# A block-sparse attention feeding a squared-ReLU MLP: the second of four batches moved from masked dense scores to gathered blocks, with its transposes and the first batch's masks on TensorE

## The chip, the core and the metric

One core of a Trainium2 chip runs the whole program in one launch. The metric is the device time in microseconds; the kernel before was timed three times and its median is 258.22 us. TensorE (PE in the profile, PEld for its weight loads), VectorE (DVE), ScalarE (ACT), GpSimd (POOL) and SyncE (SP) each work through a queue of their own, in order.

## The reference

For each of 4 batches and 8 heads there are 768 queries and keys of 64 numbers, in 24 blocks of 32. A query block may look at its neighbours, at the first and the last block and at three blocks drawn at random; the first and the last query block look at everything. The result goes through a two-layer MLP (512 to 2048 to 512).

```
scores = scale * np.matmul(q, k.transpose(0, 1, 3, 2))
mask = np.abs(blk_i - blk_j) <= window
mask = mask | (blk_i == 0) | (blk_j == 0) | (blk_i == n_blocks - 1) | (blk_j == n_blocks - 1)
for qb in range(n_blocks):
    for kb in sampled_blocks[qb]:
        mask[qb * block:(qb + 1) * block, kb * block:(kb + 1) * block] = True
scores = np.where(mask, scores, -1000000000.0)
attn = np.exp(scores - max); attn = attn / sum          # by row
x = np.matmul(attn, v) as [B * S, H * D]
out = np.maximum(x @ w_in, 0.0) ** 2 @ w_out
```

All matrix products run in bf16; the inputs and the output are float32.

## The kernel before

The work is cut into tasks: small functions that issue a few instructions each. A string, `PROGRAM`, lists every task in the order in which it is issued, with its engine as a letter (P, V, A, G, S for PE, DVE, ACT, POOL, SP) and its number; `P283/1` is task 283 on TensorE with accumulator 1 of the four PSUM accumulators `X`. A planner outside the kernel wrote that string. Each engine runs its own tasks in the order of the string, so a task that waits holds up all that stands behind it on its engine. `T_` makes a task, with the tasks that it depends on (`deps`) and the buffers that it takes and gives back.

A *unit* `u` is two heads of one batch; units 0 to 3 are batch 0, 4 to 7 batch 1, and so on. `load` (SP queue) brings queries, keys and values of a unit, `cast_qk` and `cast_v` make bf16 of them. Queries and keys are needed with the 64 numbers of a head on the partitions: for batch 0 `transp` does this on TensorE (12 small transposes for a whole unit) and `evac` copies the result out of PSUM; for the later batches `transp_dma` does it with a DMA transpose from the SP queue (line 312).

Attention exists in two forms, chosen by `SB`, the number of dense batches (2 before).

*Dense* (`attend`, batches 0 and 1): a slot is one unit, 256 queries and 256 keys. `scores` issues 4 matmuls of 256 columns (line 203; `pair` issues two matmuls that use the upper and the lower 64 rows of the array at the same time), `exps` is one ACT instruction of 128x1024 (line 360), and `masks` multiplies by a 0/1 mask on DVE (line 367). For the first 256 queries of batch 0 the mask is instead added to the scores on TensorE (`add`: 4 more matmuls, with `oh` and `R2`), since the mask tiles are not there yet. `MASKED` lists the query ranges for which `mask_tile` (TensorE) and `mask_evac` build these mask tiles. Then `values` or `values_full` multiply by V, `normalize` divides by the row sum, and the result is transposed into `xT` for the MLP: on TensorE in batch 0 (`x_transp`, `x_evac`), by DMA in batch 1 (`x_transp_dma`, line 440).

*Gathered* (`visit`, batches 2 and 3): a visit handles two groups of 64 queries, for the four units of a batch, against only the keys that the groups may see, 384 for each group. `k_gather` copies the drawn key blocks together on DVE or POOL (lines 593 to 599; block numbers are read into registers by `load_blocks`), `v_store` writes V of the batch to DRAM, `v_window` (lines 552, 556) and `v_gather` (line 579 as an indirect DMA from POOL, line 582 from SP) bring the needed rows back. `s_scores`, `s_exps` (line 623), `s_masks` (line 630), `s_values` (line 653), `s_normalize` (lines 659, 662) follow, and `s_transp` (line 666) is a DMA transpose into `xT`. Which keys, and the small masks `MKS`, are worked out once by `table_slots`, `table_spread`, `table_rows` and `table_masks`; `table_slots` is one long DVE task and `table_rows` ends by loading the block numbers of all engines.

The MLP runs in 12 tiles of 256 tokens: `hidden` (8 matmuls of 256 columns), `relu` on ACT or DVE, `square` on ACT or POOL, `output` (8 matmuls, mostly of 512 columns), `out_copy`, `store`. These tasks are laid between the attention tasks to keep TensorE busy. The weights are brought by eight `w_load` tasks on the POOL queue (pieces 0 to 3 are `w_in`, 4 to 7 `w_out`); two `loads_gate` tasks on the SP queue hold back the loads of batch 1 until pieces 6 and 7 have landed.

Of the kernel before, what the change touches and what calls it, by code (L numbers as in the profile page):

```python
# [19 lines left out]
P = 128  # L20
# [5 lines left out]
def kernel(  # L26
# [34 lines left out]
    SB, VR, KG_BUFS, VG_BUFS = 2, D + 2, 2, 3  # L61
# [404 lines left out]

    def table_places(e):
        G.iota(before, pattern=[[1, SL - 4], [-1, SL]], base=4, channel_multiplier=0, **small)
        G.iota(ids[:, 0:4], pattern=[[1, 4]], base=0, channel_multiplier=2, **small)
        G.iota(bl, pattern=[[1, 2]], base=1, channel_multiplier=2, **small)  # L470
        G.memset(ids[:, 4:5], 0.0)
        G.memset(ids[:, 5:6], float(nb - 1))
        for i in range(P // block):
            G.iota(lane[i * block:(i + 1) * block], pattern=[[0, 1]], base=0, channel_multiplier=1, **small)

    def table_slots(e):
        tmp = RT[tb["tmp"][0].at]
        n = SL - 4
        tri, eq = (tmp[0:GR, i * n * SL:(i + 1) * n * SL].rearrange("g (s z) -> g s z", z=SL) for i in range(2))
        al, sm = (tmp[0:GR, 2 * n * SL + i * 2 * SL:2 * n * SL + (i + 1) * 2 * SL].rearrange("g (a s) -> g a s", a=2) for i in range(2))  # L480
        same = tmp[0:GR, 256:256 + 2 * SL * n_rand].rearrange("g (a s r) -> g a s r", a=2, r=n_rand)
        low[0] = RT[tb["tmp"][1].at][0:D].bitcast(BF)[:, 0:5 * P].rearrange("g (s c) -> g s c", c=P)
        V.tensor_copy(out=tab.rearrange("o (g s) -> o g s", s=TS)[:, :, 0:RS],
                      in_=sb_r[:, 2 * n_rand:2 * n_rand * (nb - 1)].rearrange("o (g s two) -> o g s two", g=GR, two=2)[:, :, :, 0])
        V.memset(low[0], 0.0)
        V.tensor_copy(out=ids[:, 6:SL], in_=sb_g.rearrange("g (s two) -> g s two", two=2)[:, :, 0])
        V.tensor_tensor(out=eq, in0=ids[:, 4:SL, None].broadcast_to([GR, n, SL]), in1=ids[:, None, :].broadcast_to([GR, n, SL]), op=AOP.is_equal)
        V.scalar_tensor_tensor(out=eq, in0=before, scalar=0.0, in1=eq, op0=AOP.is_gt, op1=AOP.mult)
        V.tensor_reduce(out=dup, in_=eq, axis=AX.X, op=AOP.max)
        V.tensor_tensor(out=al, in0=ids[:, None, :].broadcast_to([GR, 2, SL]), in1=bl[:, :, None].broadcast_to([GR, 2, SL]), op=AOP.subtract)  # L490
        V.tensor_scalar(out=sm, in0=al, scalar1=-1.0, scalar2=None, op0=AOP.is_ge)
        V.scalar_tensor_tensor(out=al, in0=al, scalar=1.0, in1=sm, op0=AOP.is_le, op1=AOP.mult)
        V.tensor_tensor(out=same, in0=ids[:, None, :, None].broadcast_to([GR, 2, SL, n_rand]),
# [5 lines left out]
        V.tensor_scalar(out=dup, in0=dup, scalar1=-1.0, scalar2=1.0, op0=AOP.mult, op1=AOP.add)  # L499
        V.tensor_tensor(out=al[:, :, 4:SL], in0=al[:, :, 4:SL], in1=dup[:, None, :].broadcast_to([GR, 2, n]), op=AOP.mult)  # L500
        def spread(j, of):
# [8 lines left out]
        V.tensor_scalar(out=half, in0=lane, scalar1=float(HB), scalar2=-float(HB), op0=AOP.is_ge, op1=AOP.mult)  # L510
        V.tensor_tensor(out=lane, in0=lane, in1=half, op=AOP.add)
# [11 lines left out]
    def table_rows(e):  # L523
        V.tensor_scalar(out=idx, in0=low[1][:, P:P + GR], scalar1=float(HB), scalar2=lane, op0=AOP.mult, op1=AOP.add)
        load_blocks("POOL")
        load_blocks("DVE")
        load_blocks("SP")

    def table_masks(g0, g1, e):
        n = g1 - g0  # L530
        for c in range(3):
            copy(e, MKS[:, g0:g1, c].rearrange("p g (e a i) -> p (g e) a i", e=2, a=2) if 0 else MKS[:, g0:g1, c].rearrange("p g (e a i) -> p g e a i", e=2, a=2),
# [36 lines left out]
    def load_blocks(e):  # L569
        for g in wanted[e]:  # L570
# [94 lines left out]
    def s_transp(b, v, e):  # L665
        sy.dma_start(out=x_tile(b, v // 2 * QW)[:, :, v % 2 * P:v % 2 * P + P], in_=xtile.pop(("s", b, v)).rearrange("p a h d -> p (a h d)"), transpose=True)
# [129 lines left out]
    def prepare(u):  # L796
# [4 lines left out]
        if u >= HP:  # L801
# [5 lines left out]
            for w in (1, 0):  # L807
# [4 lines left out]
                x = T_(transp_dma, u, w, deps=[c] + old_s, put=[qc])  # L812
# [74 lines left out]
    def visit(b, v, vw, acts):  # L887
# [4 lines left out]
        parts = [T_(v_gather, b, v, i, deps=[vw, cl, tb["rows"], tb["slots"]]) for i, g in enumerate(VISITS[v]) if g]  # L892
# [4 lines left out]
        for g in [g for g in VISITS[v] if g]:  # L897
            kc[g] = T_(k_gather, b, v, g, get=[] if kc else [kb], deps=[ev[u][1, 0] for u in us] + [tb["slots"]] + list(kc.values()))
# [17 lines left out]
        nm = T_(s_normalize, b, v, deps=[va], get=[xs], put=[yb, ot])  # L916
        mu["s", b, v] = T_(s_transp, b, v, deps=[nm] + x_get(b, v // 2 * QW), put=[xs])
# [26 lines left out]
    for us in [range(b * HP, (b + 1) * HP) for b in range(B)]:  # L944
        for u in us:
            prepare(u)
        mine = [a for a in order if a[0] in us]
# [14 lines left out]
        for a in mine:  # L962
            attend(a, us[0] < HP and a[1] == 0)

    sq_of, gbuf = {}, {}
    for T in TILES:
# [3 lines left out]
        for f in range(0, NF, n_u):  # L970
# [4 lines left out]
            for part in range(parts):  # L975
# [4 lines left out]
                             put=[xb[b, c0]] if f + n_u == NF and end else []))  # L980
# [21 lines left out]
        A29 G35 P4/3 V32 P30/0 P12/2 P14/3 P9/1 P5/1 V31 P33/1 V111 P36/3 P0/2 A37 V1 V34 P102/2 V209 V46 P47/0 P106/1 A103 V48 P104/3  # L1002
        V43 A107 P44/0 G57 P7/2 V45 A105 P58/1 V54 P113/0 V59 P55/2 A114 P117/3 G41 V56 P2/1 V67 A118 P115/2 V3 P108/0 A116 V64 P127/1
        V109 P10/3 P65/3 A128 P123/2 V66 A124 P68/1 P125/3 G75 V69 V63 P92/1 P110 A126 P133/2 G76 V112 A134 P137/3 G52 S28 S42 S18 S19
        V93 S20 P88/0 A138 G38 V155 V89 P84/1 P119/2 G74 V85 A60 P86/0 P39/3 P135/1 V120 G73 A87 V40 A136 P121 P61/0 G49 P129/3 V122
        V62 G77 V70 P176/2 P170/0 P139/1 A177 G81 V130 G80 A171 V140 P146/2 P131 V132 A147 P149/3 V172 P71/0 P141 V142 A150 V72 P50/2
        P173/1 V148 P781/0 A174 P782 V178 P189/3 P783 V51 A190 V175 P90/1 P15/2 P96/2 P784 V91 A97 P183/3 V151 A785 P94/2 P179/1 V95
        A184 G787 P143/0 P774/2 V180 P775 A144 V191 G78 P186/3 P181 P776 V182 A187 P777 V145 P157/0 V778 A786 P152/3 A158 P160/1 V188
        P788/2 A161 V153 P163/0 P789 V185 A164 P790 V162 P154 P217/1 P791 A156 V159 A218 P192/0 V165 P795/3 A792 V193 S82 P166/1 S83
        V296 V219 S53 S254 A779 G794 S253 P194 P100/2 A780 P796 V195 V167 A101 P214/0 P797 G793 A215 P168 P798 V169 P211/2 V799 P824/1  # L1010
        G79 A212 P825 P196/0 G256 V216 P826 A197 P199/3 P818/2 G801 S257 P827 A200 P819 V828 P202/0 A800 S261 P228/3 P820 G22 A203
        S262 P821 V213 P812/1 S269 A229 V822 P813 G258 P220/0 A829 P814 V201 P245/2 S259 P221 A246 V198 P815 P802/3 V222 A816 P231/2
        V266 P223 P803 A232 V204 S267 P239/1 V230 P804 A224 A240 V264 S270 P242/0 P205/2 V233 S265 A243 P225/1 P206 P805 V207 A226
        S277 V274 P288/0 S436 S255 P208 P806 V227 A289 S275 V247 P11/1 P291/1 A823 P234/0 V241 P807 A292 V210 V244 P98/2 P235 V272
        P808 A99 V236 A817 S273 P298/2 V290 P248/1 P237 A299 P809 V238 S278 V293 P285/0 S279 V300 P249 A810 P830/2 V250 P831 A286 V282
        P304/3 P251 P832 V260 A305 P301/0 V252 P833 S263 V287 P852/1 A302 S334 S283 V834 P853 P846/3 G280 P313/0 V303 P854 A314 P316/2
        S281 P855 P847 A317 V856 G284 P294/0 P848 A835 S271 P295 V306 P310/1 S21 P849 G268 V297 A311 P864/2 V318 P865 S440 A850 P307/0
        V315 P866 S438 A857 P308 G851 S446 P355/3 P867 V309 A356 P322/1 V868 P858/0 P859 A323 P349/3 V357 P325/2 P860 A350 V312 P861
        P836/1 V276 A326 V351 S456 P319/3 A862 P328/2 V327 S439 P320 S447 A329 V321 P352/0 P837 S811 V324 A353 S454 P339/2 V330 P838
        A340 V354 P331/3 P342/0 A869 S385 V341 P332 P358/2 V333 P839 A343 V23 S335 G441 P359 A863 P336/3 P361/0 G443 P840 A337 P841  # L1020
        G451 A362 S622 P364/3 G449 P842 A365 P373/0 G445 S450 P843 A374 G461 P870/3 A844 S444 P367/0 V338 P871 A368 V344 S463 P872
        V347 V360 S455 V366 S442 P376/0 P345/1 A377 V363 P379/2 P346 P873 S452 V348 A380 V369 P403/0 P874 A404 V375 S464 P370/2 V378
        P400/1 P393/0 V381 P371 A401 P875 V372 S471 S448 A394 V402 P382/1 P390/2 V405 P383 A391 P387/0 P876 V384 A388 V395 S386 P406/1
# [65 lines left out]
```

## Time and profile before

| | |
|---|---|
| median of 3 runs (range) | 258.22 us (257.47 to 258.88) |
| time of the profiled run, its span | 258.88 us, 257.1 us |
| TensorE busy | 243.1 us, 95% of the span, 5265 matmuls |
| ACT, DVE, POOL busy | 183.6 us, 171.3 us, 98.8 us |
| TensorE clock granted | full speed in every slice |
| dense part: 72 `exps`, 60 `masks` | 70.6 us of ACT, 40.9 us of DVE |
| gathered part: 56 `s_exps`, 48 `s_masks` | 41.6 us of ACT, 27.6 us of DVE |
| DMA | 47.08 MB, mean 183 GB/s |

"Busy" is the time in which at least one instruction of the engine is running by the records. Matmuls are pipelined: the record of one lasts 190 to 376 ns while the next starts much earlier. The pace of TensorE is therefore read from the starts of successive rows, not from the mean duration.

### The profile page before, as it was taken

What the parts mean: (1) busy time and instruction counts of PE and PEld (TensorE: products, weight loads), DVE (VectorE), ACT (ScalarE), POOL (GpSimd) and SP (SyncE); (2) the same over time, 40 slices, a digit from 0 to 9 for tenths busy, and PEclk for the clock granted to TensorE, in tenths of its full rate; (3) what the DMA queues carried; (4) which work ended last, traced back from release to release, by engine and by line L of the source; (5) the groups of instructions that cost most, each with busy time, mean ns of one, the idle gap of its engine ahead of it and who ended that gap; (6) DMA issues with size and microseconds to landing.
All of it is one profiled execution on the core that took longest, in us unless ns stands there. A gap on an engine that the chain in (4) does not pass through costs nothing.

```text
span 257.1 us, 12061 instructions
## 1 busy us (share of the span) xinstructions
PE 243.1 (95%) x5265; PEld 182.1 (71%) x5265; DVE 171.3 (67%) x408; ACT 183.6 (71%) x217; POOL 98.8 (38%) x178
## 2 busy tenths in 40 slices
PE   7888999999999997998998999999999999999993
PEld 4667879678874677975864867866875677767683
DVE  7778988899889995969916756657536725730301
ACT  3899999998999797846783975675965286623640
POOL 3183247003316026198556314264357620412100
PEclk9999999999999999999999999999999999999999
DMA  6999989999999996999699779998474923044022
GB/s 200 374 250 207 206 205 155 270 202 252 250 281 179 197 202 153 340 229 154 188 243 202 194 174 167 251 214 199 129 206 95 189 40 60 5 121 148 23 86 83
DMA packets 64692, 47.08 MB, mean 183 GB/s; under 512 B 31567, under 2 KB 60624, under 8 KB 64640
## 3 DMA queue, kind: packets, MB, share of 16 engines
q1 hardware_dynamic: 58512, 37.82, 64.7%
q0 software_dynamic: 5440, 8.05, 16.8%
q8 instruction: 41, 0.67, 1.1%
q10 hardware_dynamic: 688, 0.46, 0.6%
q14 instruction: 11, 0.09, 0.1%
HBM read 35.51 MB, written 7.91 MB: 169 GB/s over the span
## 4 chain that ended last, share of the span: by engine, by line
PE 53%; DVE 5%; DVEq 1%; issue 1%; ACT 1%; ACTq 0%
PE X L203 49%; PE X L653 4%; DVE VB L123 1%; ACT pT L623 1%; DVEq L561 1%; DVE MKS L123 1%; DVE pT L630 1%; DVE r L709 0%; DVE KG L599 0%; DVE qc L123 0%; DVE XS L413 0%; DVE KG L593 0%; DVE XS L662 0%; DVEq L599 0%; DVE rs L410 0%
## 5 line engine op out<-in xcount | busy, mean ns | idle before, releaser
L203 PE MATMUL X<-xT,w_in_sb 64*128 64x256 bf16 x1536 | 100.8, 269 | 2.8 <-issue 1.5
L203 PE MATMUL X<-w_out_sb,g 64*128 64x512 bf16 (+3 forms) x960 | 95.2, 334 | 0.1
L203 PEld LDWEIGHTS <-w_in_sb 64*128 64x128 bf16 x1536 | 74.6, 94 | 16.0 <-issue 5.4
L360 ACT ACTIVATE pT<-X 128x1024 bf16<-128x1024 f32 x72 | 70.6, 1030 | 7.6 <-PE X L203 6.8
L623 ACT ACTIVATE pT<-X 128x768 bf16<-128x768 f32 (+1 forms) x56 | 41.6, 766 | 26.5 <-PE X L203 23.9
L203 PEld LDWEIGHTS <-g 64*128 64x128 bf16 x960 | 40.3, 94 | 26.3 <-PE X L203 0.4
L720 POOL TENSOR_TENSOR g<-r 128x1024 bf16<-128x1024 f32 (+1 forms) x20 | 31.6, 1587 | 64.4 <-ACT r L707 47.2
L707 ACT ACTIVATE r<-X 128x1024 f32<-128x1024 f32 x28 | 29.8, 1068 | 20.6 <-PE X L203 20.5
L709 DVE TENSOR_SCALAR r<-X 128x1024 f32<-128x1024 f32 x20 | 24.5, 1224 | 26.7 <-PE X L203 13.7
L367 DVE TENSOR_TENSOR pT<-pT,VG 128x1024 bf16<-128x1024 bf16 x60 | 40.9, 715 | 0.2
L718 ACT ACTIVATE g<-r 128x1024 bf16<-128x1024 f32 (+1 forms) x40 | 35.2, 899 | 2.7 <-DVE r L709 2.5
L203 PE MATMUL X<-QKT 64*128 64x256 bf16 (+1 forms) x384 | 31.6, 250 | 3.3 <-DVE XS L413 1.3
L630 DVE TENSOR_TENSOR pT<-pT,MKS 128x768 bf16<-128x768 bf16 (+1 forms) x48 | 27.6, 607 | 10.7 <-ACT pT L623 10.5
L203 PEld LDWEIGHTS <-QKT 64*128 64x128 bf16 x384 | 16.7, 95 | 9.5 <-issue 4.1
L579 POOL DMA_INDIRECT VG<-rows,idx x19 | 20.2, 1061 | 4.4 <-issue 2.6
L203 PEld LDWEIGHTS <-pT 64*128 64x128 bf16 x768 | 16.0, 94 | 1.9
L203 PE MATMUL X<-VB,pT 64*128 64x65 bf16 x768 | 17.1, 190 | 0.0
L203 PEld LDWEIGHTS <-KG 64*128 64x128 bf16 x528 | 13.8, 95 | 4.5 <-issue 0.2
L659 DVE RECIPROCAL ss<-X 128x8 f32<-128x8 f32 x12 | 2.5, 206 | 19.5 <-PE X L653 17.3
L653 PEld LDWEIGHTS <-pT 128*64 128x64 bf16 x624 | 11.9, 111 | 4.9 <-issue 3.7
L203 PE MATMUL X<-QKT,KG 64*128 64x64 bf16 x528 | 15.3, 190 | 0.1
L123 POOL CAST VB<-vs 128x768 bf16<-128x768 f32 x9 | 7.8, 869 | 16.5 <-DMA vs<-in_v_dram 16.4
(107 smaller groups left out, 210.3 us busy)
## 6 DMA issues: line engine op xcount, KB each, us to landing
vs<-in_v_dram SPq DMA_DIRECT2D x14, 384.0 KB
ks<-in_k_dram SPq DMA_DIRECT2D x13, 384.0 KB
qs<-in_q_dram SPq DMA_DIRECT2D x12, 384.0 KB
out_dram<-ys SPq DMA_DIRECT2D x9, 512.0 KB
VG<-rows SPq DMA_DIRECT2D x20, 132.0 KB
w_in_sb<-in_moe_w_in_dram POOLq DMA_DIRECT2D x4, 512.0 KB, 8.6
w_out_sb<-in_moe_w_out_dram POOLq DMA_DIRECT2D x4, 512.0 KB, 9.9
rows<-VB SPq DMA_DIRECT2D x2, 792.0 KB
```

The costliest lines, as they stand in the source:

```text
L123: (V if e == "DVE" else G).tensor_copy(out=out, in_=in_)
L203: last = nc.tensor.matmul(out(r ^ crossed), lhsT(r ^ crossed, rows), rhs(r ^ crossed, rows), skip_group_check=True, **kw)
L360: A.activation(out=pT[:, :, 0:n], in_=stile.pop(a)[:, :, 0:n], func=AF.Exp, scale=scale)
L367: V.tensor_tensor(out=pT, in0=pT, in1=m[:, None].broadcast_to([P, 2, len(cs), w]), op=AOP.mult)
L579: G.indirect_dma_start(out=to[0:RS * HB], out_offset=None, in_=pairs, in_offset=bass.IndirectOffsetOnAxis(ap=idx[0:RS * HB, g - 1:g], axis=0))
L623: A.activation(out=pT[:, :, 0:n], in_=stile.pop((u, v, gs))[:, :, 0:n], func=AF.Exp, scale=scale)
L630: V.tensor_tensor(out=pT, in0=pT, in1=m[:, None].broadcast_to([P, 2, n]), op=AOP.mult)
L653: nc.tensor.matmul(po[i * D:(i + 1) * D, h, a * VW:(a + 1) * VW], pts[g][:, h, c * D:(c + 1) * D], val, start=a == 0 and c == 0, stop=c == ...
L707: A.activation(out=to, in_=src, func=AF.Relu)
L709: V.tensor_scalar(out=to, in0=src, scalar1=0.0, scalar2=None, op0=AOP.max)
L718: A.activation(out=g, in_=r, func=AF.Square)
L720: (G if e == "POOL" else V).tensor_mul(out=g, in0=r, in1=r)
```

## The change

- `SB` goes from 2 to 1: batch 1 runs in the gathered form, so 36 dense slots go (36 `scores` and `exps`, 36 `masks`, 24 `values` tasks, 12 `normalize`) and six visits come (28 `s_scores` and `s_exps`, 24 `s_masks`, 6 each of `s_values`, `s_normalize`, `s_transp`, 11 `k_gather`, 11 `v_gather`, a third `v_store`).
- `MASKED` is empty: no mask tiles. All 36 slots of batch 0 add their mask on TensorE, where 12 did.
- Queries and keys of units 4 to 7 (`BY_PE`) are transposed by `transp` and `evac` instead of `transp_dma`.
- `s_transp` becomes 8 small transposes on TensorE, with `s_evac` as the copy to `xT`, in all three gathered batches; no DMA transposes into `xT` are left.
- The long table task is cut into `table_ids`, `table_dup`, `table_near`, `table_drawn` and `table_low`, the register loads become tasks of their own on POOL, DVE and SP, and the tables lie in the output buffers `ys`.
- `PROGRAM` is a new order: 1198 tasks instead of 1224. In it the weight pieces are issued as 7, 6, 2, 0 and later 3, 1, 5, 4; the gates stand early; the first `output` comes after more of the attention; the store of the last tile but one is behind a store of the last tile.

```
-    SB, VR, KG_BUFS, VG_BUFS = 2, D + 2, 2, 3
+    SB, VR, KG_BUFS, VG_BUFS = 1, D + 2, 2, 3
+    BY_PE = range(HP, 2 * HP)
-    MASKED = ((256, 512), (512, 768), (0, 256))
+    MASKED = ()
...
-    def table_slots(e):
...
+    def table_ids(e):
...
+    def table_dup(e):
...
+    def table_near(e):
...
+    def table_drawn(e):
...
+    def table_low(e):
...
     def table_rows(e):
         V.tensor_scalar(out=idx, in0=low[1][:, P:P + GR], scalar1=float(HB), scalar2=lane, op0=AOP.mult, op1=AOP.add)
-        load_blocks("POOL")
-        load_blocks("DVE")
-        load_blocks("SP")
...
-    def load_blocks(e):
-        for g in wanted[e]:
+    def load_blocks(g0, g1, e):
+        for g in [g_ for g_ in wanted[e] if g0 <= g_ < g1]:
...
-    def s_transp(b, v, e):
-        sy.dma_start(out=x_tile(b, v // 2 * QW)[:, :, v % 2 * P:v % 2 * P + P], in_=xtile.pop(("s", b, v)).rearrange("p a h d -> p (a h d)"), transpose=True)
+    def s_transp(b, v, buf, e):
+        xs = xtile.pop(("s", b, v))
+        pt = tile_of(buf)[:, :, 384:512].bitcast(BF).rearrange("p r (a i) -> p r a i", i=D)
+        for a in range(HP):
+            for r, rows in enumerate(HALVES):
+                nc.tensor.transpose(pt[:, r, a], xs[rows, a].rearrange("p h d -> p (h d)"), identb[rows, rows])
+        xtile["t", b, v] = pt
+
+    def s_evac(b, v, e):
+        to = x_tile(b, v // 2 * QW)[:, :, v % 2 * P:v % 2 * P + P]
+        copy(e, to.rearrange("q a (r i) -> q r a i", r=2), xtile.pop(("t", b, v)))
...
-                x = T_(transp_dma, u, w, deps=[c] + old_s, put=[qc])
+                if u in BY_PE:
+                    hb = Buf("X")
+                    t = T_(transp, u, w, ALL, hb, deps=[c], get=[hb], put=[qc])
+                    x = T_(evac, u, w, ALL, deps=[t] + old_s, put=[hb])
+                else:
+                    x = T_(transp_dma, u, w, deps=[c] + old_s, put=[qc])
...
-        nm = T_(s_normalize, b, v, deps=[va], get=[xs], put=[yb, ot])
-        mu["s", b, v] = T_(s_transp, b, v, deps=[nm] + x_get(b, v // 2 * QW), put=[xs])
+        nm = T_(s_normalize, b, v, deps=[va], get=[xs])
+        xt = T_(s_transp, b, v, yb, deps=[nm], put=[xs])
+        mu["s", b, v] = T_(s_evac, b, v, deps=[xt] + x_get(b, v // 2 * QW), put=[yb, ot])
...
-            attend(a, us[0] < HP and a[1] == 0)
+            attend(a, True)
...
     PROGRAM = """
-        A29 G35 P4/3 V32 P30/0 P12/2 P14/3 P9/1 P5/1 V31 P33/1 V111 P36/3 P0/2 A37 V1 V34 P102/2 V209 V46 P47/0 P106/1 A103 V48 P104/3
...
+        P2/0 V100 P0/1 P17/2 A36 A39 G42 P43/3 P11/2 P40/2 G50 V1 V44 P37/1 A38 P35 V53 S18 P54/3 A41 P8/1 V64 P95/1 V55 P93/2 P16/3
...
```

More of the change, by code (lines that the diff above doesn't have):

```diff
@@ L465, in table_load, with table_scratch @@
         sy.dma_start(out=sb_g, in_=sampled_blocks.bitcast(I32)[1:nb - 1].rearrange("(g a) w -> g (a w)", a=2))
+    def table_scratch():
+        tmp = [YS[b_.at] for b_ in tb["tmp"]]
+        n = SL - 4
+        tri, eq = (tmp[0][0:GR, i * n * SL:(i + 1) * n * SL].rearrange("g (s z) -> g s z", z=SL) for i in range(2))
+        al, sm = (tmp[0][0:GR, 2 * n * SL + i * 2 * SL:2 * n * SL + (i + 1) * 2 * SL].rearrange("g (a s) -> g a s", a=2) for i in range(2))
+        same = tmp[0][0:GR, 256:256 + 2 * SL * n_rand].rearrange("g (a s r) -> g a s r", a=2, r=n_rand)
+        return n, eq, al, sm, same, tmp[1][0:D].bitcast(BF)[:, 0:5 * P].rearrange("g (s c) -> g s c", c=P)
     def table_places(e):
@@ L897, in visit @@
         for g in [g for g in VISITS[v] if g]:
-            kc[g] = T_(k_gather, b, v, g, get=[] if kc else [kb], deps=[ev[u][1, 0] for u in us] + [tb["slots"]] + list(kc.values()))
+            kc[g] = T_(k_gather, b, v, g, get=[] if kc else [kb], deps=[ev[u][1, 0] for u in us] + [tb["ids"]] + list(kc.values()) + (sum((cq[u, w] for u in (2, 3) for w in (0, 1)), []) if b == SB else []))
             kc[g].blocks = g, ("POOL", "DVE")
@@ L935 @@
     t = T_(table_load, deps=[])
-    p = T_(table_places)
-    tmp = tb["tmp"] = [Buf("r"), Buf("r")]
-    tb["slots"] = T_(table_slots, deps=[t, p], get=tmp)
+    tmp = tb["tmp"] = [Buf("ys"), Buf("ys")]
+    p = T_(table_places, get=tmp)
+    i_ = tb["ids"] = T_(table_ids, deps=[t, p])
+    for e_ in ("POOL", "DVE", "SP"):
+        T_(load_blocks, 0, 4, deps=[i_])
+        T_(load_blocks, 4, nb, deps=[i_])
+    d_ = T_(table_dup, deps=[i_])
+    n_ = T_(table_near, deps=[i_])
+    w_ = T_(table_drawn, deps=[d_, n_])
+    l_ = T_(table_low, deps=[w_])
     hb = Buf("X")
-    t = T_(table_spread, hb, deps=[tb["slots"]], get=[hb], put=tmp)
+    t = T_(table_spread, hb, deps=[l_], get=[hb], put=tmp)
     tb["rows"] = T_(table_rows, deps=[t], put=[hb])
@@ L979 @@
                              get=[] if part else [ht, rb, gb, hb],
-                             put=[xb[b, c0]] if f + n_u == NF and end else []))
+                             put=[xb[b, c0]] if end else []))
             rr = T_(relu, T, f, deps=[hd[-1]], put=[hb, ht])
@@ L1006 @@
[L1006 to L1009, printed above, removed]
```

127 lines of the change are left out of this document (65 added, 62 removed).

## The prediction

> **What bounds the kernel now.** I read the page's busy line first, then busy time by stretch, then the starts on TensorE's timeline.
>
> ```profile
> PE 243.1 (95%) x5265; PEld 182.1 (71%) x5265; DVE 171.3 (67%) x408; ACT 183.6 (71%) x217; POOL 98.8 (38%) x178
> ...
> 0.00:4.17 4.17, 2.96 (x28) 2.06 (x30) 3.00 (x14) 1.79 (x2) 1.59 (x12) 1.00 0.51 142
> 4.17:55.00 50.83, 47.27 (x1017) 37.19 (x1015) 42.86 (x91) 46.99 (x56) 18.49 (x31) 1.00 1.09 240
> 55.00:95.00 40.00, 39.12 (x887) 29.50 (x881) 36.95 (x86) 36.66 (x40) 9.98 (x15) 1.00 1.11 230
> 95.00:150.00 55.00, 50.82 (x1202) 39.95 (x1199) 39.28 (x106) 38.43 (x46) 31.39 (x58) 1.00 0.95 204
> 150.00:253.30 103.30, 102.94 (x2152) 73.37 (x2148) 48.89 (x114) 59.50 (x76) 37.36 (x63) 1.00 0.58 133
> 253.30:257.10 3.80, 0.00 (x0) 0.00 (x0) 0.29 (x1) 0.18 (x1) 0.00 (x0) 1.00 0.13 37
> ```
>
> The second part has for each stretch its length, then the busy time and instructions of PE, PEld, DVE, ACT and POOL, the granted clock, the DMA share and GB/s. TensorE is the bound of the whole, and ACT beside it until 95 us (47.0 of 50.8 us, 36.7 of 40). TensorE without any matmul in flight: 3.56, 0.88, 4.18 and 0.36 us in the four middle stretches. A record lasts 190 ns or more, so this hides short waits; the true waits come from the paces below.
>
> ```profile
> 11.50 0.91 PE L398 MATMUL X<-VB,pT 128*128 128x65 bf16 x24
> 12.34 0.28 PE L203 MATMUL X<-QKT 64*128 64x256 bf16 x2
> ...
> 37.35 0.22 PE L427 MATMUL X<-identb,xq 64*128 64x64 bf16 x4
> 37.41 0.60 PE L203 MATMUL X<-xT,w_in_sb 64*128 64x256 bf16 x8
> ...
> 39.83 1.47 PE L203 MATMUL X<-xT,w_in_sb 64*128 64x256 bf16 x24
> 41.14 0.66 PE L203 MATMUL X<-QKT 64*128 64x256 bf16 x8
> ...
> 44.17 0.40 PE L203 MATMUL X<-QKT 64*128 64x256 bf16 x4
> 44.39 0.54 PE L203 MATMUL X<-VB,pT 64*128 64x65 bf16 x24
> 44.76 0.61 PE L203 MATMUL X<-xT,w_in_sb 64*128 64x256 bf16 x8
> ...
> 146.53 0.34 PE L203 MATMUL X<-QKT,KG 64*128 64x64 bf16 x12
> 146.70 2.11 PE L203 MATMUL X<-xT,w_in_sb 64*128 64x256 bf16 x32
> ...
> 205.73 1.47 PE L203 MATMUL X<-xT,w_in_sb 64*128 64x256 bf16 x24
> 207.13 0.95 PE L653 MATMUL X<-VG,pT 128*64 128x65 bf16 x48
> 208.02 1.05 PE L203 MATMUL X<-xT,w_in_sb 64*128 64x256 bf16 x16
> ...
> 227.04 1.89 PE L203 MATMUL X<-w_out_sb,g 64*128 64x512 bf16 x16
> 228.77 0.49 PE L203 MATMUL X<-xT,w_in_sb 64*128 64x256 bf16 x6
> ```
>
> The difference of two starts over the count is the pace: 55 ns for a matmul of 256 columns (24 in 1.31 us, 4 in 0.22), 108 for 512 (16 in 1.73), 15 for the 65 columns of `values` (24 in 0.37) and for a transpose (4 in 0.06), 14 for gathered scores (12 in 0.17), 18.5 for `s_values` (48 in 0.89). The second run of 24 `hidden` matmuls takes 1.40 us where the first took 1.31: entering `s_values` costs 0.09. A `values_full` takes 0.84 (11.50 to 12.34); with the same price of entry I count 0.93.
>
> Times their counts: `hidden` 1536, 83.8 us; `output` 704 wide and 256 narrow, 76.1 and about 7; scores and masks 354, 19.5; `values` 768, 11.5; `values_full` 8 tasks, 7.4; gathered scores 624, 8.8; `s_values` 624 with 12 entries, 12.6; 144 transposes, 2.2; small things 1.5. Sum 230.4. With 4.2 before the first task of the order (28 warm-up matmuls) and 3.8 after the last matmul that leaves 257.1 - 238.4 = 18.7 us of **waits**. Spread as the idle time is, 7.4 lie before 55 us, 1.8 up to 95, 8.7 up to 150 and 0.7 after.
>
> **Part by part: TensorE's work.** Taken away: 36 dense score tasks, 144 x 55 ns = 7.9; 24 `values` tasks, 576 x 15 = 8.6; the mask tiles, 18 x 55 = 1.0; together 17.5. Added: 24 mask additions, 96 x 55 = 5.3; 28 `s_scores`, 312 x 14 = 4.4; six `s_values`, 312 x 18.5 and 6 x 0.09 = 6.3; 96 transposes of queries and keys and 144 of results, 240 x 15 = 3.6; together 19.6. Net **+2.1**, and on an engine without slack all of it counts.
>
> For the transposes the Trainium skill ("TensorE: Matmul & The Clock Gate", Part 4) gives about 275 ns each in a kernel, for a full 128x128; 240 of them would by this estimate be 66 us instead of 3.6. The start spacing of the rows above disagrees with that as a pace.
>
> **The other engines' work.**
>
> ```profile
> L360 ACT ACTIVATE pT<-X 128x1024 bf16<-128x1024 f32 x72 | 70.6, 1030 | 7.6 <-PE X L203 6.8
> L623 ACT ACTIVATE pT<-X 128x768 bf16<-128x768 f32 (+1 forms) x56 | 41.6, 766 | 26.5 <-PE X L203 23.9
> L367 DVE TENSOR_TENSOR pT<-pT,VG 128x1024 bf16<-128x1024 bf16 x60 | 40.9, 715 | 0.2
> L630 DVE TENSOR_TENSOR pT<-pT,MKS 128x768 bf16<-128x768 bf16 (+1 forms) x48 | 27.6, 607 | 10.7 <-ACT pT L623 10.5
> ...
> 10.14 7.54 ACT L360 ACTIVATE pT<-X 128x1024 bf16<-128x1024 f32 x8 [0.35 <-PE X L203]
> ...
> L312 SPq DMA_TRANSPOSE QKT<-qc x24: 1210/1296/3300, 39.5 to 166.2; - x24
> L666 SPq DMA_TRANSPOSE xT<-XS x12: 1190/1210/1827, 132.4 to 227.7; - x12
> ```
>
> ACT: 36 x 0.94 (8 in 7.54) = 34 us of exponentials go and 28 x 0.77 = 21 come. DVE: all 60 masks (41) go, 24 x 0.61 = 15 come. SP: 8 + 18 transposes of about 1.25 us go, 32 us of its queue; fewer windows and gathers come. POOL gets more casts and gathers, but at 38% has room. None of this counts where TensorE's streaming covers it; it counts in the waits. The table tasks (DVE, some 7 us in pieces) and the register loads are costed at nothing under batch 0, where DVE was busy 42.9 of 50.8 us and loses 24 masks, 17 us; without that cover they would delay `normalize`, and TensorE with it, by up to a piece each, some 2 us. On the DMA queues the loads of batch 1 and its store move forward, next to the weight pieces, in a stretch with a share of 1.09 already; eight DMA transposes leave it. I cost that at nothing as long as casts stand several us ahead of TensorE; the third rival prices it if not. So the waits, stretch by stretch:
>
> Start, 7.4 now. ACT sets the pace here. By the place where TensorE has streamed 41 us, the old order has given ACT 37 exponentials, the new one 36, six copies from PSUM in place of three mask exponentials, and the same MLP work to about 1 us. Fewer DVE masks help nothing that ACT feeds. I take 7.5, bounds 6 and 10. The upper one covers two new places: a key transpose of unit 2 stands on TensorE behind a POOL cast, itself queued behind the cast of V of unit 0, and the weight pieces 0, 3 and 1 are issued late on POOL, between casts, with `hidden` right behind them.
>
> Up to 95 us, 1.8 now: the ACT-bound dense batch 1 is gone; the gathered form asks ACT for about 7 us in 10 (38.4 of 55 in the stretch from 95 us). I take 0 and put what comes there into the next term.
>
> The first gathered batch, 8.7 now.
>
> ```profile
> 97.39 1.05 PE L203 MATMUL X<-xT,w_in_sb 64*128 64x256 bf16 x16 [0.38 <-DMA xT<-XS]
> ...
> 100.21 0.18 DVE L410 RECIPROCAL rs<-X 128x4 f32<-128x4 f32 x1 [2.66 <-ACT pT L360]
> 100.91 0.28 PE L203 MATMUL X<-QKT 64*128 64x256 bf16 x2 [1.02 <-DVE XS L413]
> ...
> 120.29 2.62 DVE L123 CAST VB<-vs 128x768 bf16<-128x768 f32 x1
> ```
>
> DVE does nothing for 2.66 us while it loads block numbers, and TensorE stops for 1.02; a DMA transpose is late by 0.38; a cast of V on DVE stands 2.62 us ahead of what TensorE needs. The new order has the register loads in six pieces under batch 0, where DVE lost 24 masks, no such DMA, and more of the casts on POOL. What stays are the gather's own latencies and stops "on issue". I take 4.2, about half; bounds 1 and 13 (all of it, and the chain of the third rival).
>
> The rest: 0.7 in 103 us now, so 1.2 over the 180 us that follow. The new wait is `s_transp`: on TensorE, in order, behind DVE's `s_normalize`. All later matmuls queue behind it. The reciprocal and product take 0.9 us, and the new order, added up with the paces above, leaves 1.2 to 5 us of streaming before each of the 18, so a wait arises only if DVE is late; 0.7 in all, up to 18 masks of 0.61 = 11 if it always is. 1.9 together.
>
> Waits 7.5 + 4.2 + 1.9 = 13.6, **5.1 less**.
>
> **The end.**
>
> ```profile
> 253.72 0.37 ACTq L776 DMA_DIRECT2D out_dram<-qs  x1
> ```
>
> The last issue ends at 254.09, 3.0 us before the span does. In the new order SP has a 512 KB store and two small ones behind a store that waits for a copy made at the very end: two more issues of 0.37 give **+0.8** (0 if they overlap, 2.8 if 512 KB at the mean 183 GB/s go first).
>
> Sum: +2.1 - 5.1 + 0.8 = -2.2, a span of 254.9. The profiled run took 258.88 for 257.1; it lies 0.66 above the median of 258.22, from which I count: **256.0 us**. In general the time is 242.4 + waits.
>
> **Rivals.**
> *Nearly no waits after the start.* The stretch after 150 us shows that gathered visits can run with 0.7 in 103 us. Then 7 + 1.5 + 1 = 9.5 and 251.9 us. Against it: the first visits also have loads, stores and casts around them.
> *No change:* the waits of the first gathered batch only move forward, 14.5 to 17 in all, 256.9 to 259.4, say 258.2. For it: DMA share is 1.09 where these visits now lie, against 0.95.
> *Slower, by the chain of V through DRAM at the first visit of batch 1.*
>
> ```profile
> 104.10 0.59 SPq L538 DMA_DIRECT2D rows<-VB  x1
> ...
> 110.27 0.80 SPq L552 DMA_DIRECT2D VG<-rows  x2
> ...
> 121.72 0.22 PE L653 MATMUL X<-VB,pT 128*64 128x65 bf16 x1
> ...
> DMA to landing us min/median/max: 3.5/4.2/6.0
> ```
>
> From the store to the first `s_values` before: 17.6 us. The new order, by the same paces, has 13.3 us of streaming between them. If the chain needs what it took, TensorE waits 4.3 more: 260.3 us; it decides from 3.5 us late. Against it: store to first window 6.2, one gather 6.0 at most, so 12 to 13 would do.
> *Transposes occupy TensorE for as long as their records last.*
>
> ```profile
> L305 PE MATMUL X<-identb,qc 64*128 64x64 bf16 x96 | 3.7, 199 | 1.6 <-ACT pT L360 0.8 <-DVE qc L123 0.6
> ```
>
> 240 x 0.19 is 46 instead of 3.6: about 298 us. The 96 of this row have only 3.7 us busy in all, so next to nothing speaks for it. It is the Trainium skill's figure above taken as a pace.
>
> **How the numbers follow.** Forecast 0.40 (its own range 254 to 256.9), nearly no waits 0.13, no change 0.24, slower by the chain 0.22, long transposes 0.01. About 0.5%, 1.3 us, is what a measurement of this kernel can tell from no change: faster 0.53, same 0.24, slower 0.23. The range 251.5 to 261 leaves out the lower half of the second case, the chain if it is much later than before, and the last: some 0.18.
>
> **What would show it.** TensorE: 5487 matmuls counted (222 more), transposes 15 ns apart, a streaming sum near 232.5 us. ACT busy less by some 12 us, DVE by 20 or more, the idle time of TensorE in the first 55 us about as now and no stretch later with more than 2 us. Wrong if the first gathered visit starts more than 17 us after its store, if TensorE waits for `XS` at line 662 many times, if `hidden` of the first tile waits for weights, or if ACT falls behind at the start.

## The result, and the profile after

The changed kernel takes 270.07 us (median of 4 runs, 268.49 to 271.84), the kernel before, run beside it, 258.55 (257.47 to 260.48): **ratio 1.0439, 95% interval 1.0343 to 1.0535, slower**. The forecast was 256.0 with a range up to 261. The profiled execution took 270.87 us for a span of 269.0.

The page of the changed kernel: busy time, and the clock that TensorE was granted, in 40 slices.

```profile
PE 247.9 (92%) x5487; PEld 186.8 (69%) x5487; DVE 153.8 (57%) x411; ACT 178.1 (66%) x219; POOL 111.2 (41%) x233
...
PEclk9998999799799999999999999999999999999999
```

Every other engine is less busy than before, or has room; TensorE has the 5487 matmuls that were forecast, but its share fell from 95% to 92%, and its clock dips in the slices that begin at 20, 47 and 67 us. The same stretches of both kernels, first the one after, then the one before (columns as in the prediction):

```profile
0.00:40.00 40.00, 33.94 (x676) 27.48 (x678) 21.96 (x73) 33.14 (x39) 19.30 (x48) 0.96 0.99 254
40.00:70.00 30.00, 23.89 (x615) 21.61 (x611) 18.81 (x59) 18.96 (x26) 15.95 (x33) 0.89 0.88 196
70.00:150.00 80.00, 77.46 (x1749) 56.09 (x1744) 56.28 (x136) 55.22 (x68) 44.73 (x86) 1.00 0.94 225
150.00:263.93 113.93, 112.60 (x2459) 81.65 (x2456) 56.59 (x145) 70.63 (x89) 31.24 (x68) 1.00 0.48 114
263.93:269.00 5.07, 0.00 (x0) 0.00 (x0) 0.18 (x1) 0.19 (x1) 0.00 (x0) 0.92 0.58 207
```

```profile
0.00:40.00 40.00, 35.23 (x702) 27.69 (x704) 32.88 (x80) 33.98 (x41) 16.87 (x33) 1.00 1.01 233
40.00:70.00 30.00, 29.37 (x686) 24.56 (x684) 26.01 (x48) 28.47 (x33) 7.92 (x15) 1.00 1.13 234
70.00:150.00 80.00, 75.56 (x1736) 56.45 (x1733) 63.18 (x169) 61.43 (x70) 36.66 (x68) 1.00 1.00 210
```

From 40 to 70 us TensorE idles 6.1 us where it idled 0.6, and runs at 0.89 of its clock; from 70 to 150 it idles less than before (2.5 for 4.4). I laid the paces of the prediction over every task of both traces; what a task takes beyond its pace is a wait. The difference of the two spans, 269.0 - 257.1 = 11.9 us, is then

| | us |
|---|---|
| streaming (with entries to `s_values`) | +2.2 |
| before the first task | +0.4 |
| waits: up to 40 us +1.9, 40 to 70 us +8.5, 70 to 150 us -1.5, later -0.2, less 0.6 of entries already in the first row | +8.0 |
| after the last matmul (5.07 for 3.80) | +1.3 |

So most of the loss lies in one stretch of 30 us. Who TensorE waited for, from the waits of the changed kernel (us in total, times, longest), and its timeline at the two largest:

```profile
PE X L204 <- issue: 6.6, 3, 3.3
PE X L306 <- DVE qc L124: 1.9, 3, 1.1
PE X L667 <- DVE pT L644: 1.5, 2, 1.2
```

```profile
45.64 0.28 PE L204 MATMUL X<-VB,pT 64*128 64x65 bf16 x7
48.40 0.43 PE L204 MATMUL X<-VB,pT 64*128 64x65 bf16 x17 [2.47 <-issue]
...
62.52 1.15 PE L204 MATMUL X<-xT,w_in_sb 64*128 64x256 bf16 x18
66.99 2.53 PE L204 MATMUL X<-xT,w_in_sb 64*128 64x256 bf16 x22 [3.32 <-issue]
```

Both stops cut a task in two: 7 of the 24 matmuls of one `values`, then nothing for 2.5 us, then the other 17, which wait for no data that the first seven did not have. "Issue" says that no semaphore held TensorE. The stretch before the first stop and the stop itself, then the three spells at half clock and the 3.41 us ahead of the first of them:

```profile
42.00:45.74 3.74, 3.74 (x128) 3.51 (x128) 3.39 (x8) 3.13 (x4) 2.33 (x5) 1.00 1.17 295
45.74:48.40 2.66, 0.19 (x10) 0.06 (x6) 0.53 (x1) 1.02 (x1) 2.66 (x6) 1.00 1.24 207
```

```profile
15.65:19.06 3.41, 1.75 (x52) 1.47 (x52) 1.41 (x4) 2.31 (x3) 3.41 (x6) 1.00 0.90 143
19.06:22.47 3.41, 3.41 (x56) 2.56 (x50) 0.62 (x2) 2.96 (x3) 3.18 (x13) 0.50 1.11 171
49.78:53.19 3.41, 3.41 (x58) 2.89 (x54) 1.74 (x11) 2.46 (x3) 0.00 (x0) 0.50 0.87 145
66.85:70.26 3.41, 3.27 (x41) 2.74 (x42) 0.00 (x0) 0.38 (x1) 2.21 (x9) 0.50 1.12 257
```

Each spell lasts 3.41 us and costs half of what TensorE streams in it, 1.7, 1.7 and 1.6 us: 5.0 us beside the 5.8 us of the two stops. The spells begin in steps of 3.41 us (49.78 - 19.06 is nine of them, 66.85 - 49.78 is five). In all the traces of this case, leaving out their first 3.4 us and what follows the last matmul, each such step in which TensorE had no matmul in flight for 1.9 us or more, 15 of them, was followed by one at half clock. With 1.3 to 1.9 us idle it went both ways: 1.66 us ahead of 19.06 us was enough, 1.87 us in a run below was not. The Trainium skill ("TensorE: Matmul & The Clock Gate", Part 1) has half clock after an idle window of about 3.4 us; here 1.9 us without matmuls inside such a step were always enough. The other three executions had mean granted clocks of 0.987 to 0.991, against 0.980 here; by estimate, at 1.7 us of some 267 for each spell, that is one or two spells instead of three.

The first of the three has no stop on issue before it. Its cost of 1.7 us is nearly all of the 1.9 us lost before 40 us. A load of queries was late, DVE's cast of them waited for it, and TensorE for the cast:

```profile
17.06 0.48 DVE L124 CAST qc<-qs 128x512 bf16<-128x512 f32 x1 [2.09 <-DMA qs<-in_q_dram]
17.59 0.29 PE L306 MATMUL X<-identb,qc 64*128 64x64 bf16 x8 [1.07 <-DVE qc L124]
```

What was missing is in the DMA rows of the page (packets, MB, share of 16 engines):

```profile
q8 instruction: 43, 0.70, 1.2%
```

Queue 8 moves with TensorE's count of instructions: 43 packets of 16 KB for 10,974 matmuls and weight loads, 255 each, or some **128 matmuls to a packet**. The DMA queues between 41.9 and 45.9 us, then between 45.9 and 46.9:

```profile
q1 hardware_dynamic: 1107, 0.85, 69.6%
q0 software_dynamic: 310, 0.32, 47.4%
q14 instruction: 1, 0.01, 0.5%
```

```profile
q0 software_dynamic: 187, 0.19, 111.8%
q8 instruction: 1, 0.02, 5.8%
q1 hardware_dynamic: 9, 0.00, 2.2%
```

Counted in the trace, a packet starts soon after TensorE has passed a multiple of 128 matmuls (plus an offset of 95 at both stops), and TensorE stops when it has issued the 128 that follow and the packet is not there. At 41.9 us it passed such a point; the 128 matmuls after it, transposes, `values` and mask additions, took 3.8 us (the first of the rows with the clock begins 0.1 us later: x128 in 3.74); the packet started only at 45.92, ended at 46.86, and matmuls began again 1.54 us later. At 59.5 it was 3.9 us of matmuls against a packet that started at 64.7.

### The profile page after: what moved, and what is told of

It reads as the page before. It is cut to its first block, busy times and chain, and to the rows that moved or that the text cites. A ratio compares the mean times of both kernels' runs of the same rounds, so it can differ in the third digit from the quotient of the medians.

```text
span 269.0 us, 12715 instructions
## 1 busy us (share of the span) xinstructions
PE 247.9 (92%) x5487; PEld 186.8 (69%) x5487; DVE 153.8 (57%) x411; ACT 178.1 (66%) x219; POOL 111.2 (41%) x233
## 4 chain that ended last, share of the span: by engine, by line
PE 78%; DVE 6%; issue 4%; DMA 4%; ACT 2%; SPq 2%; POOL 1%; DVEq 0%; POOLq 0%; ACTq 0%
PE X L204 67%; PE X L667 7%; DMA ks<-in_k_dram 4%; DVE pT L644 2%; PE X L399 2%; ACT pT L361 2%; PE X L306 1%; DVE MKS L124 1%; DVE qc L124 1%; PE X L684 1%; POOL qc L124 1%; SPq L313 1%; DVE VB L124 1%; DVE KG L613 0%; SPq L570 0%
## 5 line engine op out<-in xcount | busy, mean ns | idle before, releaser
L204 PEld LDWEIGHTS <-w_in_sb 64*128 64x128 bf16 x1536 | 74.7, 95 | 18.7 <-issue 4.0
L637 ACT ACTIVATE pT<-X 128x768 bf16<-128x768 f32 (+1 forms) x84 | 62.1, 762 | 37.7 <-PE X L204 32.5
L644 DVE TENSOR_TENSOR pT<-pT,MKS 128x768 bf16<-128x768 bf16 (+1 forms) x72 | 42.9, 635 | 7.5 <-ACT pT L637 7.5
L743 POOL TENSOR_TENSOR g<-r 128x512 bf16<-128x512 f32 (+1 forms) x14 | 21.3, 1528 | 54.8 <-ACT r L730 34.1
L361 ACT ACTIVATE pT<-X 128x1024 bf16<-128x1024 f32 x36 | 34.8, 1045 | 7.7 <-PE X L204 6.3
L732 DVE TENSOR_SCALAR r<-X 128x1024 f32<-128x1024 f32 x17 | 20.8, 1223 | 14.5 <-PE X L204 14.5
L204 PE MATMUL X<-QKT 64*128 64x256 bf16 (+1 forms) x288 | 22.6, 237 | 1.1 <-DVE QKT L124 0.6
L204 PE MATMUL X<-QKT,KG 64*128 64x64 bf16 x792 | 22.6, 190 | 0.0
L667 PE MATMUL X<-VG,pT 128*64 128x65 bf16 x792 | 19.7, 197 | 1.8 <-DVE pT L644 1.5
L613 POOL COPY KG<-QKT 128x64 int32 x90 | 19.2, 258 | 0.0
L204 PE MATMUL X<-R,oh 64*128 64x256 bf16 x144 | 18.2, 278 | 0.0
L124 DVE COPY xT<-X 128x512 bf16<-128x512 bf16 (+1 forms) x24 | 8.6, 360 | 12.7 <-PE X L684 9.3
## 6 DMA issues: line engine op xcount, KB each, us to landing
w_in_sb<-in_moe_w_in_dram POOLq DMA_DIRECT2D x4, 512.0 KB, 10.6
```

Source lines behind the costliest of these rows:

```text
L124: (V if e == "DVE" else G).tensor_copy(out=out, in_=in_)
L204: last = nc.tensor.matmul(out(r ^ crossed), lhsT(r ^ crossed, rows), rhs(r ^ crossed, rows), skip_group_check=True, **kw)
L361: A.activation(out=pT[:, :, 0:n], in_=stile.pop(a)[:, :, 0:n], func=AF.Exp, scale=scale)
L613: eng.tensor_copy(out=rows[:, :, :, r_ * w:(r_ + 1) * w], in_=src[:, :, :, bass.ds(at[r_] * w, w)])
L637: A.activation(out=pT[:, :, 0:n], in_=stile.pop((u, v, gs))[:, :, 0:n], func=AF.Exp, scale=scale)
L644: V.tensor_tensor(out=pT, in0=pT, in1=m[:, None].broadcast_to([P, 2, n]), op=AOP.mult)
```

## The experiments

Theory A: the packet is late because the weight pieces' transfers (issued at 40 to 57.5 us) are in its way. B: the instructions there are too short, whatever the traffic. C: the loss is SP's queue, which stood for 18.7 us at the store of V, waiting for its cast. Times differ between chips (the kernel before had medians of 255.8 to 261.7 beside these runs), so ratios to it are compared; without the experiment's edit the ratio is 1.0439.

**Weight pieces early.**
```diff
-  ... P194 G84 P788 ... P15/0 G82 S220 ... V34 G86 G292 ... V272 G85 P259 ...
+  ... G67 G81 G84 G82 G86 G85 S239 ...
```


> The changed kernel with the weight pieces 3, 1, 5 and 4 issued right behind piece 0 on POOL (some 23 to 26 us instead of 40.2 to 57.5); nothing else moved. Theory A (TensorE runs out of instructions at 45.7 and 63.4 us because the transfers of these pieces delay the 16 KB instruction packet): both stops on issue, 2.5 and 3.3 us, fall below 1 us, and with the half clock behind each the time falls by 5 to 9 us, to 262 to 266. Theory B (the instructions there are short, and the packet comes too late whatever the traffic): stops within 1 us of now, 269 to 272. Theory C (the loss is SP's queue behind the store of V, 18.7 us): 269 to 272, SP's wait unchanged.

Ratio 1.0679 (1.0593 to 1.0765): slower still. The first stop went: its packet started 1.9 us after the point instead of 4.0, and the 128 matmuls, partly at half clock, lasted 5.0 us instead of 3.8. The second fell from 3.3 to 2.2 us, its packet starting 3.6 us after the point instead of 5.2. That is the direction of A, short of its size, but the pieces now delayed the loads of batch 1; the waits have a new first row:

```profile
PE X L306 <- POOL qc L124: 5.8, 5, 3.3
```

Where the weights lie in time only chooses who is late; A in its narrow form falls.

**More traffic in the kernel before.**
```diff
+    def extra_load(i, e):
+        G.dma_start(out=spare[i], in_=wov[:, 0:NF // NWP])
-  ... G258 P220/0 ...
+  ... G258 G1224 G1225 G1226 G1227 G1228 G1229 P220/0 ...
```


> The kernel before with six more transfers of one weight piece each (512 KB, from the weights to DRAM, nothing reads them), issued on POOL at some 43 us; the output is the same. Theory A: stops on issue of 1 to 3 us appear on TensorE between 47 and 62 us, where the trace of before has 0.7 to 2 us of slack between packet and use, with the half clock behind them; 260.5 to 266 us. Theory B: the packets of before hold longer matmuls (4.7 us and more each), so no stop over 0.5 us; 258 to 260, as loads have slack.

Ratio 1.0565 (1.0456 to 1.0674), 14.5 us, beyond what either had. But no stop cuts a task; TensorE waited for data:

```profile
PE X L203 <- DMA QKT<-qc: 11.3, 2, 6.0
```

It tells nothing on packets; it shows that 3 MB more at 43 us find no free DMA time before batch 1's transposes.

**Half a packet more, and a whole one.** The clean test: the same program, cut into packets at other places. The second kernel has 64 in place of 32.
```diff
+    for _ in range(32):
+        pair(lambda i: X[NX - 1][:, i, 0:32], lambda i, rows: warm[rows, 0:P], lambda i, rows: warm[rows, 0:32], start=True, stop=True)
```


> The changed kernel with 64 more warm-up matmuls of 32 columns at the start (about 1 us while TensorE waits for the first keys), which moves every later instruction by half a packet of 128 matmuls. If the stops are the end of an instruction packet (A and B), they stay at the same count from the start of TensorE's queue, so they come 64 matmuls earlier or later in the program, not in the 8th matmul of the values of unit 2 and the 19th of that hidden run; packets of 128 matmuls then last 3.7, 4.0 and 3.1 us by the paces where they now last 3.8 and 3.7, so the time need not fall: 265 to 274. If a stop belongs to its place in the program (a wait that the trace doesn't show), it stays there.

> The changed kernel with 128 more warm-up matmuls of 32 columns, a whole instruction packet. If the stops are ends of packets, the cuts between packets fall on the same places in the program as in the changed kernel, so the stops come back in the 8th matmul of the values of unit 2 and the 19th matmul of that hidden run, 128 later in the count from the queue's start, and the gain of the 64 is gone: 268 to 272 (1 us of it for the longer start). If the 64 helped for another reason (a warmer TensorE, a later start), 128 help as much or more: 261 to 264.

Half a packet: **1.0252** (1.0151 to 1.0352). A whole one: **1.0674** (1.0589 to 1.0759). More warm-up of the same kind first gains 1.8% and then loses it and more. The gain alone is at the edge of the noise, the 4% between the two kernels is clear of it. With half a packet no stop on issue over 1.8 us is left, and the first over 1 us is at another place, in a transpose (the profiled execution took 267.1 us for a median of 263.0, with half clock from 9.3 to 19.5 us, so only places are read from it):

```profile
50.81 0.28 PE L308 MATMUL X<-identb,qc 64*128 64x64 bf16 x7
52.20 0.24 PE L308 MATMUL X<-identb,qc 64*128 64x64 bf16 x5 [1.11 <-issue]
```

With a whole one they are back where they were, 7 of 24 and 18 matmuls into the same two runs:

```profile
45.53 0.28 PE L204 MATMUL X<-VB,pT 64*128 64x65 bf16 x7
47.73 0.43 PE L204 MATMUL X<-VB,pT 64*128 64x65 bf16 x17 [1.92 <-issue]
...
61.94 1.15 PE L204 MATMUL X<-xT,w_in_sb 64*128 64x256 bf16 x18
66.51 2.53 PE L204 MATMUL X<-xT,w_in_sb 64*128 64x256 bf16 x22 [3.43 <-issue]
```

The stop belongs to the packet's end, not to the task: from the start of TensorE's queue the first lies behind 863 matmuls in the changed kernel and behind 991 = 863 + 128 with a whole packet more. The stop shown with half a packet lies behind 991 too, which is 64 matmuls further into the program. This is shown.

**Is the packet late by traffic?** Over nine traces of these kernels, the median time from TensorE's passing the point to the packet's start, by the DMA share around that moment: below 0.1, 0.25 us (41 packets); around 0.4, 0.7 us (35); around 0.8, 1.7 us (67); around 1.2, 2.8 us (90), the longest 5.0. With 1.1 us of transfer and 1.4 to the next matmul, a packet of 128 matmuls must by these medians last 2.8 us on an idle DMA and 5.3 on a full one. A direct test, nine transfers of 512 KB as above, put where nothing else waits for a DMA:
```diff
-  ... G1104 P1116 ...
+  ... G1104 G1198 G1199 G1200 G1201 G1202 G1203 G1204 G1205 G1206 P1116 ...
```


> The changed kernel with nine transfers of 512 KB (weights to DRAM, nothing reads them) issued on POOL at some 237 us, where no engine waits for a DMA any more. In the changed kernel the instruction packets there start 0 to 0.8 us after TensorE has crossed into the last packet it has. If traffic delays them: 2 to 3.5 us, and a stop of 0.5 to 2 us on issue where the packet lasts 3.9 us (some 259 to 263 us); the time 0.5 to 3 us longer. If they have a way of their own: 0 to 1 us as now, and no stop.

The three packets under the extra traffic started 2.6, 2.9 and 3.2 us after the point, where they had started 0.0, 0.0 and 0.8 us after it, and a stop appeared where the changed kernel has none:

```profile
263.51 0.86 PE L204 MATMUL X<-w_out_sb,g 64*128 64x128 bf16 x32 [1.37 <-issue]
```

The one run took 271.2 us. So traffic delays the packet, shown; B's half is next.

**Fewer, longer instructions.**
```diff
-    FULL = (0, 256)
+    FULL = (0, 256, 512)
```


> The changed kernel with the values of the last 256 queries of batch 0 computed by 24 matmuls of 128 rows instead of 48 of 64, as those of the first 512 already are: 96 matmuls fewer just where the first stop lies, 0.2 us more streaming for each of the four units, the same result. If the stops come from packets of 128 matmuls that are used up faster than the next arrives (the measured 3.5 to 5.3 us from the crossing to the first use of the new packet while the DMA engines are busy), the first stop goes with its half clock, and the packets behind it are cut elsewhere: about half of the stops, 263 to 267 us. If the stops depend on the traffic alone: 270 to 272.

Ratio 1.0328 (1.0222 to 1.0433), so the gain from 1.0439 is not clear of the noise. The profiled execution, the shortest of four at 261.9 us, has no slice at a lower clock and no wait on issue over 0.5 us:

```profile
PEclk9999999999999999999999999999999999999999
```

```profile
PE X L667 <- issue: 1.8, 4, 0.5
```

Both stops are gone in it, with 0.8 us more streaming. The longest of the four took 268.4 us at a mean granted clock of 0.984, so stops may have come back there; no trace shows it. Nor does the run alone tell density from place, since 96 matmuls fewer also move the cuts between packets. The length of the packets tells. The kernel with full rows and an earlier store, under "What is left" below, has the same matmuls, and after its point at 41.3 us the packet comes as late as in the changed kernel:

```profile
41.30:47.05 5.75, 5.53 (x128) 4.89 (x128) 5.15 (x13) 4.17 (x6) 5.09 (x11) 1.00 1.22 242
```

Its packet started 3.9 us after the point (4.0 in the changed kernel), at a DMA share of 1.22 (1.17). But the 128 matmuls last 5.7 us instead of 3.8, and TensorE stops for 0.3 us instead of 2.5. At the second place the packet started 4.3 us after the point (5.2), the matmuls last 5.9 us (3.9), and the stop is 0.6 us (3.3). So it takes both for a long stop, short matmuls and traffic.

> As e9, and the transposes of queries and keys by 128x128 instead of two 64x64 halves: another 96 matmuls fewer in the batch with gathers and as many in batch 0, for the same time on TensorE if one takes 30 ns where two halves took 2 x 15. By the packet reckoning one third of the stops is left: 260 to 264 us. If a full transpose costs TensorE more than two halves (190 ns as its record lasts, 130 of them more than before hidden): 275 or more. If density doesn't matter: as e9.


```diff
-            for r, rows in enumerate(HALVES):
-                nc.tensor.transpose(pt[:, r, n], src[rows, i].rearrange("p t d -> p (t d)"), identb[rows, rows])
+            nc.tensor.transpose(pt[:, n], src[:, i].rearrange("p t d -> p (t d)"), identb)
```
Ratio 1.0268 (1.0185 to 1.0351), no clear gain over the last, because a full transpose is not as cheap as I assumed:

```profile
42.41 0.51 PE L305 MATMUL X<-identb,qc 128*128 128x128 bf16 x6
42.86 0.28 PE L204 MATMUL X<-QKT 64*128 64x256 bf16 x2
```

Six take 0.45 us, 75 ns each; twelve halves take 0.17 (43.56 to 43.73 us in the changed kernel). 96 of them cost 4.4 us more than the 192 halves.

**SP's queue and the start.** Two edits of the order, each in a kernel of its own.
```diff
-  ... G292 P771 P772 A773 P755/2 V227 P756 ...
+  ... G292 G227 P771 P772 A773 P755/2 P756 ...
```


> The changed kernel with the cast of V of unit 4 on POOL, behind its first gather of keys (some 50 us), instead of on DVE behind the table's masks (56.5 us), so that the store of V can go at some 51 us instead of 58.05, and with it the loads queued behind it on SP. Theory C: the waits of 60 to 100 us shrink, 265 to 268 us. Theory A: the store no longer falls on piece 4; the second stop may shrink by 1 to 2 us, the first stays, 267 to 271. Theory B: 269 to 272.

```diff
-  G48 G61 P51/3 ...
+  G61 G48 P51/3 ...
```


> The changed kernel with one exchange on POOL: the cast of the keys of unit 2, on which a transpose on TensorE waits, ahead of the cast of V of unit 0. If the start is late for that cast, the wait of 0.4 us at 11.5 us goes, the idle spells of the first 20 us shrink by 0.5 to 1.5 us, and the time by the same: 268.5 to 270. If the start is bound by ACT, as the prediction had it, nothing moves: 269.5 to 271. The stops at the ends of packets stay in both.

The store of V moved by 10.6 us, and the times did not: 1.0429 (1.0348 to 1.0510) and, for the keys, 1.0531 (1.0428 to 1.0634), although the wait for them at 11.5 us went. SP's issue of the store, after and with the cast on POOL:

```profile
58.05 0.34 SPq L552 DMA_DIRECT2D rows<-VB  x1
```

```profile
47.46 0.34 SPq L552 DMA_DIRECT2D rows<-VB  x1
```

C and the late keys fall as causes while the stops stand. Combining does not add up as long as the packets decide:

> The changed kernel with three edits at once: 64 more warm-up matmuls of 32 columns (half an instruction packet), the cast of V of unit 4 on POOL, and the keys of unit 2 cast ahead of V of unit 0. Alone the first gave 263.0 and the second 266.9 against 270.1. If both worked on the same stops, they don't add: 262 to 264. If the second worked on SP's queue and the loads behind it, they add: 258 to 261, about the time of before; below that only if the start is shortened too.

1.0416 (1.0332 to 1.0501): stops of 1.7, 1.5 and 3.3 us came back at other ends of packets. That the earlier loads changed the traffic there is likely, but not tested.

> As e10, and the cast of V of unit 4 on POOL (266.9 against 270.1 alone). If that gain was SP's queue and the loads behind it, it adds: 257 to 261, about as fast as the kernel before. If it was the place of the stops, it does not: 260 to 264.

1.0280 (1.0160 to 1.0400), as without the cast.

**One part alone: the masks.** In the kernel before, `attend(a, us[0] < HP)` in place of `us[0] < HP and a[1] == 0`, and the 24 product tasks struck from the order.

> The kernel before with one part of the change alone: the masks of all of batch 0 added on TensorE, so 24 more mask additions (96 matmuls of 256 columns) and 24 fewer products on DVE (17 us). By the prediction's paces TensorE gets 5.3 us more. If all of it counts: 262 to 264. If DVE's relief takes waits of the start away, as much as the prediction hoped for in all: 258 to 261. If the 96 matmuls also move the cuts between packets to places with short matmuls: 263 to 267.

Ratio 1.0151 (1.0069 to 1.0232). In the profiled execution the span is 3.9 us longer: 5.3 of streaming, 1.9 less of waits (0.5 the other way at the end), with no stop on issue in a task. In it DVE's relief gives a third of the masks' price back.

**What is left.** The 512 KB store of the second tile of batch 3 ahead of the one that waits, on top of the full rows; then both casts as well.
```diff
-  ... P1174 S1167 P1175 P1184 P1185 P4/3 V1176 S1129 P6/0 ...
+  ... P1174 S1129 S1167 P1175 P1184 P1185 P4/3 V1176 P6/0 ...
```


> The kernel of e9 (values of the last 256 queries by full rows) with the 512 KB store of the second tile of batch 3 issued ahead of the store that waits for the last copies, some 5 us earlier. If the end is part of what is left: 1.0 to 1.5 us after the last matmul less, so 3.8 instead of 5.1, and 260.5 to 265. If the transfers then only overlap the last output's: the same end, 261.9 to 266.5.

> As e13, and the cast of V of unit 4 on POOL and the keys of unit 2 cast ahead of V of unit 0. If start and SP's queue hold what is left: 257 to 260, no slower than the kernel before. If what is left is the added streaming (2.1 us, and 0.8 for the full rows): 260 to 264, still 1 to 2% slower.

The first, 1.0264 (1.0122 to 1.0407): the end fell from 5.07 to 3.76 us, as the prediction's two queued issues would have it, within the noise of the whole.

```profile
258.94:262.70 3.76, 0.00 (x1) 0.00 (x0) 0.19 (x1) 0.20 (x1) 0.00 (x0) 0.96 0.42 140
```

The second: **1.0066 (1.0008 to 1.0124)**, 263.2 us beside 261.7 of the kernel before. Four edits that leave the change itself alone take its loss from 4.4% to 0.7%. No version tried beats the kernel before. How much the two casts do here, where the longest wait on issue is 1.0 us, stays open: the intervals of the last two touch.

## Why the prediction was wrong

*The step that failed* is the sum of the waits, 13.6 forecast, 26.7 found (18.7 + 8.0). The rest of the sum held: 242.4 + 26.7 is 269.1, and the 1.0 us up to the measured 270.1 is 0.4 before the first task, 0.5 more at the end than forecast and 0.1 of streaming. The term that failed most is the start, everything up to 55 us: 7.5 forecast with 10 as its upper bound, some 13.5 found, which is 7.4 + 1.9 up to 40 us, 2.5 for the first stop and 1.7 for the half clock behind it. The term up to 95 us, taken at 0, got the second stop and its half clock. Behind both is one step: the prediction took the traffic of loads and weight pieces at nothing "as long as casts stand several us ahead of TensorE". The list of those who wait for a DMA did not have TensorE's own instruction packets in it. Stops "on issue" stood in the prediction as something that merely stays. Nor was there a term for the clock, which was 1.00 everywhere before; its three spells cost 5.0 us.

The rows to see it with were there: the page of before lists queue 8, and two short stops on issue in its trace begin their next matmul 1.4 us behind the end of a packet, as the long stops do. The fetch was just in time:

```profile
58.58 0.40 PE L203 MATMUL X<-QKT 64*128 64x256 bf16 x4 [0.27 <-issue]
...
64.16 1.05 PE L203 MATMUL X<-xT,w_in_sb 64*128 64x256 bf16 x16 [0.31 <-issue]
```

The change put 96 transposes of 15 ns, `values` of 15 ns and gathered scores of 14 ns into a stretch whose DMA share I had quoted as 1.09. At the two stops 128 matmuls lasted 3.8 and 3.9 us, where packets of the old order, counted the same way, lasted 5.2 and more between 35 and 75 us; by the medians above a packet under that load needs 5.3. The Trainium skill ("Runtime: NRT & Kernel Launch", Instruction fetch mechanics) has the blocks of 16 KiB and calls their fetch mostly hidden; here it was not.

*Right:* 5487 matmuls and +2.1 of streaming (2.2 found); transposes 14 ns apart, so the long-transpose rival is out (it was priced at the 0.19 us of the records, not at the 275 ns that stand above it); the direction at the first gathered visits (70 to 150 us, -1.5, though forecast about -4.5); `s_transp` behind DVE costs next to nothing (-0.2 after 150 us); the end (+0.8 forecast, +1.3 found).

*Wrong in size without consequence:* ACT fell by 5.5 us, not 12, DVE by 17.4, not 20; neither engine set the pace after 40 us. The key transpose behind a POOL cast, named as a danger of the start, did wait 0.4 us, but taking that wait away moved nothing.

*The rivals:* "slower by the chain of V" had the right sign for a reason that was not it. Its sign came true (the first `s_values` at 77.1 us is 19.1 after the store at 58.05, over the 17 named), but with the store 10.6 us earlier the time stayed. Late weight pieces were named as a danger for `hidden`; `hidden` never waited for them.

## What to carry to other kernels

TensorE's instructions come by the same DMA engines as the data, 128 matmuls at a time and one packet ahead: where the DMA share is near 1, any 128 matmuls in a row that stream in less than some 5 us are a risk, so count short matmuls per packet before moving transposes to TensorE. An idle time "on issue" in the middle of a task is the sign, and moving all instructions by half a packet is a cheap test for it. A stop of 1.9 us or more that falls into one step of the clock is paid again, with up to 1.7 us of half clock.

## What the hardware showed that I had not expected

A new order's time depends on where its instruction packets happen to be cut: the same work with 64 more tiny matmuls in front is 1.8% faster, with 128 more 2.3% slower than without. Transposes of half height follow each other at 14 ns, so two take 28; a full one takes 75 ns.
